# Router logits from the normalised attention output, turned by VectorE, in place of nine columns of values

## The chip, the core and the metric

The kernel runs on one core of a Trainium2 chip. The core has five engines that run side by side and meet at semaphores: TensorE (PE, with its weight loads shown apart as PEld), VectorE (DVE), ScalarE (ACT), GpSimd (POOL) and SyncE (SP, which here only issues DMAs). The metric is device time in microseconds for one execution, the median of the runs. Everything is float32.

## The reference

Attention over 8 batches, 8 heads, 576 positions and 64 features is followed by a mixture of 8 experts that sends each token to one expert:

```python
scores = q @ k.T / sqrt(D); cum = cumsum(max(s, 0))
scores = where(causal, -1e9, scores + min(-(cum[i] - cum[j]), 0))
x = softmax(scores) @ v                       # (B, H, S, D) -> (B, S, 512)
logits = x @ w_gate                           # 8 per token
local_gate = sigmoid(x @ w_local)             # 1 per token
e = argmax(logits) if s == 0 or local_gate < 0.5 else e of the token before
out = softmax(logits)[e] * (relu(x @ w1[e]) @ w2[e])      # 512 -> 1024 -> 512
```

A token's row of x is needed twice: for its nine router values (eight logits and the locality gate), and in its expert.

## The kernel before

**Attention.** A slot is one pair of heads; there are 32, four (`HP`) to a batch. The loop over `n` writes out by hand what each engine gets. In slot `n`, PE computes the scores of pair `n` in four units (`scores`, L896), each into a bank `ps` from a pool of three pairs of banks; ACT takes the exponential (L897), POOL masks the diagonal (L882). Then PE multiplies the weights of pair `n - 1` with the values (`values`, L923). The result `po` has 64 query rows of one head in partitions 0 to 63 and of the other in 64 to 127, and it is made in two parts, chunks 0 to 5 (`NJA`) and 6 to 8. `po` has one buffer for each part. `evacuate` on DVE takes the reciprocal of the sum column (L929), writes x into `xb` (L931) and, before the change, the nine router columns into `lb` (L933).

**Where the router values come from.** The product is linear, so the kernel before appends nine columns to the 64 of each head's values: v times the router weights of that head. A value row in `vg` has `VW` = 75 columns: 64 of v, nine router columns, and two for sums. To make them, v is also loaded in a turned layout (`vT`, `load_vT`), PE multiplies it with `wbd` (`value_logits`, L837, bank `vwp`), DVE turns the result into `tk` (L841, L843), and `weigh_logits` (L865) or `weigh_heads` (L879) multiplies it with the key weights. After a group of two batches `sums` adds the four pairs (L941) and `product` adds the two head halves on PE with the 0/1 matrix `fold` (L193, bank `lp`).

**The router's steps.** `codes` finds the best expert, `turn1` and `turn2` carry an expert along the tokens that keep it, `ranks` (PE) and `rows` give each token its row in a table in device memory, `gates` the probability, and 18 `scatter` calls a group put the rows of x there with indirect DMAs on POOL (L309), each behind a small operation on `gap` (L308) that waits for a given evacuation. Which step stands in which slot is written by `plan(slot, place, f)`: place 0 is behind score unit 1, place 1 behind the first part of the values, place 3 at the slot's end. `xb` has four buffers, one per batch, so a batch's buffer is rewritten four batches later, when its scatters have landed. For the last group these steps run inside the experts' first unit (`Experts.run`, the table `todo`), and scatters that are left over (`puts`) go one to each piece of the first layer.

**The experts.** After slot 32 the table's rows are fetched in units of up to 256 rows; PE runs the first layer (L539, L530) and the second (L563), while the weights of the next expert stream in.

**Other work in a slot.** `weigh` (L855) multiplies the v of the next batch with key weights on DVE, in three pieces; `load_qk` and `load_v` issue DMAs on SP. In the first two slots the order is special: v is weighed pair by pair (`weigh_heads` over `PARTS`).

Of the kernel before, what the change touches and what calls it, by code (L numbers as in the profile page):

```python
# [32 lines left out]
VW = DH + E + 3  # L33
WR = 16
NJ = S // DH
# [23 lines left out]
def kernel(  # L59
# [6 lines left out]
    vT: bass.AP,  # L66
# [3 lines left out]
    wbd: bass.AP,  # L70
# [15 lines left out]
    with ExitStack() as main:  # L86
        router = Router(main, tc, ident, table)
        experts = Experts(main, tc, w1, w2, out, table, router)
        with ExitStack() as early:
            attention(early, tc, q, k, vm, vt, vT, s, wbd, ident, recs, wend, router, experts)  # L90
        experts.run(recs, wend, out_of)
# [18 lines left out]
class Router:  # L110
# [8 lines left out]
    def constants(self):  # L119
        nc, ident, table = self.nc, self.ident, self.table  # L120
        self.fold = self.t("fold", [P, P])
        for h in range(2):
            nc.gpsimd.tensor_tensor(self.fold[:, h * DH : h * DH + DH], ident[:, :DH], ident[:, DH:], op=Alu.add)
# [59 lines left out]

    def t(self, name, shape, dt=F32):
        return self.const.tile(shape, dt, name=name)
# [4 lines left out]
    def product(self, g, ls, banks):  # L190
        flat = banks("lp")[:, 0, : NC * (E + 1)]
        ps = flat.rearrange("p (c e) -> p c e", e=E + 1)
        self.nc.tensor.matmul(flat, lhsT=self.fold, rhs=ls.rearrange("p c e -> p (c e)"),  # L193
                              start=True, stop=True)
        self.g[g] = {"l": ps}
# [217 lines left out]
class Experts:  # L413
    def __init__(self, ctx, tc, w1, w2, out, table, router):
# [11 lines left out]
        self.p_x = self.x_stack.enter_context(tc.tile_pool(name="p_x", bufs=2 * GB, side="right"))  # L426
        self.puts = []
# [148 lines left out]
    def run(self, recs, wend, out_of):  # L576
# [14 lines left out]
        def late_rows():  # L591
# [7 lines left out]
            (0, 2): [lambda: router.product(last, self.ls, self.banks), lambda: router.codes(last),  # L599
# [93 lines left out]
def attention(ctx, tc, q, k, vm, vt, vT, s, wbd_in, ident, recs, wend, router, experts):  # L693
# [9 lines left out]
    p_v = pool("p_v", 1)  # L703
    p_e = pool("p_e", 2)
    p_x = experts.p_x
    p_sm = pool("p_sm", 1)
# [6 lines left out]
    ins, vTs, es, xs, lgs = {}, {}, {}, {}, {}  # L713
# [16 lines left out]
    def load_vT(b):  # L730
        if b >= B:
            return
        vTs[b] = p_v.tile([P, HP, NB * P], F32, name="vTb")
        nc.sync.dma_start(vTs[b], vT[b])

# [11 lines left out]
    wbd = once.tile([P, HP, 2 * WR], F32, name="wbd")  # L747
    load_qk(1)
    nc.sync.dma_start(wbd, wbd_in)
    vTs[0] = p_v.tile([P, HP, NB * P], F32, name="vTb")  # L750
    for a0, a1 in PARTS:
        hs = slice(2 * a0, 2 * a1)
        nc.sync.dma_start(vTs[0][:, a0:a1], vT[0][:, a0:a1])
        nc.sync.dma_start(va[:, :NF, hs], vm[0][:, :, hs])
        nc.sync.dma_start(va[TL:, NF, hs], vt[0][:, hs])
    for n in range(2, 4):
        load_qk(n)
    wk1 = once.tile([P, B, G1, H], F32, name="wk1")
# [66 lines left out]
    def value_logits(b, a0=0, a1=HP):  # L825
        if b >= B:
            return
        vTb = vTs[b] if a1 < HP else vTs.pop(b)
        m, n = min(a1 - a0, HP - 1), 2 * WR
        ps = banks("vwp")  # L830
        pm = ps[:, 0, : m * NB * n].rearrange("p (a c e) -> p a c e", a=m, c=NB)
        pl = ps[:, 1, : NB * n].rearrange("p (c e) -> p c e", c=NB)
        for hp in range(a0, a1):
            at = vTb[:, hp, :].rearrange("p (c r i) -> p r c i", c=NB, r=4)
            for r in range(4):
                d = slice(32 * r, 32 * r + 32)
                mm(pm[d, hp - a0] if hp - a0 < m else pl[d], lhsT=wbd[:, hp, :], rhs=at[:, r], start=True, stop=True)  # L837
        if a0 == 0:
            lgs[b] = p_sm.tile([P, NB, HP, n], F32, name="tk")
        tk = lgs[b]  # L840
        nc.vector.transpose(tk[:, :, a0 : a0 + m].rearrange("p c a e -> p a c e"), pm)  # L841
        if a1 - a0 > m:
            nc.vector.transpose(tk[:, :, HP - 1], pl)  # L843

# [15 lines left out]
    def weigh_logits(b):  # L860
        if b >= B:
            return
        tk = lgs[b].rearrange("p c a (h e) -> p c (a h) e", h=2)
        for g, c in enumerate((G1, NB)):
            nc.vector.tensor_tensor(vgs[b % 2][g][:, :, :, DH : DH + E + 1].rearrange("p c h e -> p (c h) e"),  # L865
                                    tk[:, :c, :, : E + 1].rearrange("p c h e -> p (c h) e"),
                                    (wk1, wk2)[g][:, b].rearrange("p c h -> p (c h)").unsqueeze(2)
                                    .to_broadcast([P, c * H, E + 1]), op=Alu.mult)

    def weigh_heads(a0, a1, logits):  # L870

        hs = slice(2 * a0, 2 * a1)
        for g, c in enumerate((G1, NB)):
            to, of = vgs[0][g][:, :, hs, :DH], va[:, :c, hs]
            if logits:
                to = vgs[0][g][:, :, hs, DH : DH + E + 1]
                of = lgs[0].rearrange("p c a (h e) -> p c (a h) e", h=2)[:, :c, hs, : E + 1]
            w = (wk1, wk2)[g][:, 0, :, hs].unsqueeze(3).to_broadcast(list(to.shape))
            nc.vector.tensor_tensor(to, of, w, op=Alu.mult)  # L879
# [29 lines left out]
    def values(n, j0, j1):  # L909
# [4 lines left out]
        if (g, "l") not in xs:  # L914
            xs[g, "l"] = p_sm.tile([P, HP, NC, E + 1], F32, name="lb")
        xb, lb = xs[b], xs[g, "l"]
# [34 lines left out]
    for g in range(NG):  # L951
# [6 lines left out]
        if g == NG - 1:  # L958
            break
# [670 lines left out]
```

## Time and profile before

| what | value |
|---|---|
| median of 3 runs | 756.76 us (756.22 to 757.38) |
| profiled execution, its own time | 757.18 us |
| its span on the core | 755.4 us |
| first expert matmul | 232.75 us |
| busy PE, DVE, ACT, POOL | 98%, 31%, 22%, 28% of the span |
| granted TensorE clock | 0.997 |

The span is that of the program's own instructions, and 1.8 us of the profiled execution lie around it. A line of the profile names an engine, the source line, the operation and `out<-in` by the program's tile names; x is a count. A float32 matmul stands in the profile as two instructions, so counts of matmuls are twice those of the code. PE's busy time includes modelled ends of overlapping matmuls; for durations of a block, the start of the next block minus its own start is used.

### The profile page before, as it was taken

The page shows a single profiled execution, that of the slowest core. Times are in us where ns is not written, and L with a number is a line of the kernel's source. Part 1 is how long each engine was busy: PE and PEld are TensorE (multiplying, and loading weights), DVE is VectorE, ACT ScalarE, POOL GpSimd, SP SyncE. Part 2 cuts the span into 40 slices and gives each one's busy share as a digit, 9 for nine tenths or more (in the row PEclk, how much of TensorE's full clock was granted, in tenths as well). Part 3 has the DMA queues.
Part 4 walks back from the last instruction along what each step waited for, and adds up shares of the span by engine and source line. Part 5 has one row for each costly group of instructions (what it writes and reads, how often), then busy time and mean ns, then how long its engine had stood idle before and what let it go on. Part 6 is the DMA issues. An engine that isn't in the chain of part 4 may idle for free.

```text
span 755.4 us, 15982 instructions
## 1 busy us (share of the span) xinstructions
PE 743.3 (98%) x6463; PEld 511.8 (68%) x6463; DVE 236.7 (31%) x677; ACT 163.2 (22%) x319; POOL 214.7 (28%) x455
## 2 busy tenths in 40 slices
PE   8999999999999999999999999999999999999996
PEld 5888888887789567567567365637644676637674
DVE  4655655655656372101100411041132001050110
ACT  4544444443541011011011010201110111101110
POOL 2562376675657245340100011010101001000110
PEclk9999999999999999999999999999999999999998
DMA  8766457659677896598545979996999965899000
GB/s 279 263 244 228 159 174 273 207 176 315 217 254 271 270 373 215 210 422 233 213 177 169 374 246 392 339 378 242 423 321 383 410 220 216 297 391 354 29 14 33
DMA packets 56580, 196.50 MB, mean 260 GB/s; under 512 B 11693, under 2 KB 32429, under 8 KB 47280
## 3 DMA queue, kind: packets, MB, share of 16 engines
q1 hardware_dynamic: 49696, 175.28, 65.4%
q0 software_dynamic: 6800, 20.09, 7.0%
q8 instruction: 53, 0.87, 0.5%
q14 instruction: 31, 0.25, 0.1%
HBM read 174.73 MB, written 20.88 MB: 259 GB/s over the span
## 4 chain that ended last, share of the span: by engine, by line
PE 94%; DVE 2%; POOL 1%; DMA 1%; issue 1%; ACT 0%; POOLq 0%; ACTq 0%
PE yp L563 34%; PE hp L539 30%; PE po L923 13%; PE ps L896 11%; PE hp L530 4%; PE vwp L837 1%; DMA table<-xb,idx 1%; PE warm L770 1%; POOL e L882 0%; DVE vg L855 0%; DVE xb L931 0%; ACT e L897 0%; POOL table L309 0%; DVE mi L227 0%; PE pos L261 0%
## 5 line engine op out<-in xcount | busy, mean ns | idle before, releaser
L563 PE MATMUL yp<-w2b,hT 128*128 128x512 f32 (+2 forms) x752 | 259.3, 593 | 0.0
L539 PE MATMUL hp<-xT,w1b 128*128 128x256 f32 (+1 forms) x1216 | 233.1, 352 | 0.0
L539 PEld LDWEIGHTS hp<-xT,w1b 128*128 128x128 f32 x1216 | 206.2, 190 | 32.4 <-issue 7.3
L563 PEld LDWEIGHTS yp<-w2b,hT 128*128 128x128 f32 (+2 forms) x752 | 107.9, 167 | 141.0 <-issue 139.6
L568 POOL DMA_INDIRECT out_dram<-y,gi x37 | 36.2, 978 | 416.9 <-DVE y L566 386.7
L541 ACT ACTIVATE hT<-hp 128x256 f32<-128x256 f32 (+1 forms) x152 | 54.1, 356 | 430.2 <-PE hp L539 430.2
L566 DVE TENSOR_SCALAR y<-yp,gi 128x512 f32<-128x512 f32 x37 | 27.6, 746 | 309.9 <-PE yp L563 303.6
L897 ACT ACTIVATE e<-ps 128x768 f32<-128x768 f32 (+1 forms) x128 | 97.6, 836 | 108.3 <-PE ps L896 107.2
L923 PE MATMUL po<-vg,e 128*64 128x75 f32 x3200 | 113.3, 229 | 0.0
L923 PEld LDWEIGHTS po<-vg,e 128*64 128x64 f32 x3200 | 107.2, 136 | 3.8 <-issue 0.8
L896 PE MATMUL ps<-qb,kb 64*128 64x192 f32 (+4 forms) x768 | 99.8, 403 | 3.4 <-DVE u L206 1.9
L896 PEld LDWEIGHTS ps<-qb,kb 64*128 64x128 f32 x768 | 68.5, 188 | 35.1 <-ACT e L897 9.7
L309 POOL DMA_INDIRECT table<-xb,idx x72 | 75.7, 1051 | 28.2 <-issue 25.9
L882 POOL TENSOR_SCALAR_AFFINE_SELECT e<-e 128x256 f32<-128x256 f32 (+1 forms) x160 | 64.1, 427 | 52.3 <-ACT e L897 51.2
L550 DVE STREAM_TRANSPOSE hT<-hs 32x256 f32<-32x256 f32 x64 | 27.9, 436 | 74.9 <-ACT hs L532 74.0
L929 DVE RECIPROCAL recs<-po 128x12 f32<-128x12 f32 x64 | 13.2, 207 | 75.0 <-PE po L923 74.8
L931 DVE TENSOR_TENSOR xb<-po,recs 128x384 f32<-128x384 f32 x64 | 29.3, 458 | 7.1 <-DMA table<-xb,idx 4.8
L855 DVE TENSOR_TENSOR vg<-va,wk 128x1024 f32<-128x1024 f32 (+1 forms) x21 | 29.6, 1412 | 0.7 <-DMA va<-in_vm_dram 0.7
L509 DVE STREAM_TRANSPOSE xT<-xq 128x1024 f32<-128x1024 f32 (+1 forms) x23 | 23.7, 1032 | 15.2 <-DMA xq<-table 14.9
L530 PE MATMUL hp<-w1b,xT 128*32 128x512 f32 (+1 forms) x224 | 28.3, 594 | 0.0
L530 PEld LDWEIGHTS hp<-w1b,xT 128*32 128x32 f32 (+1 forms) x224 | 8.1, 114 | 17.7 <-issue 17.6
L308 POOL COPY gap<-recs 1x1 f32<-1x1 f32 x39 | 8.5, 217 | 29.4 <-DVE recs L929 29.2
(235 smaller groups left out, 188.1 us busy)
## 6 DMA issues: line engine op xcount, KB each, us to landing
w1b<-in_w_dram SPq DMA_DIRECT2D x29, 2048.0 KB
w2b<-in_w_dram SPq DMA_DIRECT2D x29, 2048.0 KB
kb<-in_k_dram SPq DMA_DIRECT2D x32, 288.0 KB
qb<-in_q_dram SPq DMA_DIRECT2D x32, 288.0 KB
vTb<-in_vT_dram SPq DMA_DIRECT2D x7, 1280.0 KB
xq<-table SPq DMA_DIRECT2D x56, 130.0 KB
va<-in_vm_dram SPq DMA_DIRECT2D x7, 1024.0 KB
w1b<-in_w_dram SPq DMA_DIRECT2D x4, 512.0 KB
```

The lines of the kernel that those rows point to most:

```text
L309: put = self.nc.gpsimd.indirect_dma_start(out=self.halves, in_=src, element_offset=0, in_offset=None, out_offset=bass.IndirectOffsetOnAxis ...
L530: mm(ps[d, :], lhsT=xT[:, k, d], rhs=self.ws[l][0][:, k, c * 512 : c * 512 + 512], start=(k == 0), stop=(k == DK - 1))
L539: mm(ps[:, :w], lhsT=self.ws[ls[0]][0][:, k, c * P : c * P + P], rhs=xT[:, k, :w], start=(k == 0), stop=(k == DK - 1))
L541: nc.scalar.activation(self.hT[u][:, c, :w], ps[:, :w], Act.Relu)
L563: mm(ps[d, :], lhsT=hT[:, k, n * P + d.start : n * P + d.stop], rhs=self.ws[l][1][:, k, :], start=(k == 0), stop=(k == FK - 1))
L568: put = nc.gpsimd.indirect_dma_start(out=self.out[:, :], out_offset=bass.IndirectOffsetOnAxis(ap=gi.bitcast(I32)[:, n, 0:1], axis=0), in_= ...
L855: nc.vector.tensor_tensor(vgs[b % 2][g][:, c0:c1].rearrange("p c h e -> p (c h) e")[:, :, :DH], va[:, c0:c1].rearrange("p c h e -> p (c h) ...
L882: nc.gpsimd.affine_select(out=ap, in_=ap, compare_op=Alu.is_ge, fill=0.0, base=base, pattern=n, channel_multiplier=-1)
L896: mm(ps[:, h, at : at + z - a], lhsT=kb[d, key : key + P], rhs=qb[d, a:z], start=True, stop=True)
L897: nc.scalar.activation(e, ps, Act.Exp, scale=scale)
L923: mm(po[d, j - j0, :], lhsT=weights_of(n, c, j, h), rhs=vg[:, c, 2 * hp + h, :], start=(c == 0), stop=(c == last))
L931: nc.vector.tensor_tensor(xb[:, j0:j1, :, 32 * hp : 32 * hp + 32], po[:, :, :DH].rearrange("p j (g i) -> p j g i", g=2), rec[:, :, 0].unsq ...
```

## The change

The values lose the nine router columns (`VW` is 66), and with them `vT`, `value_logits`, `weigh_logits`, `lb`, `sums` and `fold` go. Instead, after each pair's second evacuation `turn` transposes the pair's x on DVE in 32x32 blocks into `xt`. `product` multiplies that with the router weights `wx`: 32 matmuls a group (four pairs, two halves of 32 features, two batches, two runs of five chunks) that accumulate in one bank, each batch and run in its own group of 32 columns. `logits` turns the bank back and copies the nine values to where `codes` reads them. For the last group the product is split by batch: the first half in slot 29, the second in the experts' first unit. `codes` to `turn2` move to later places, some scatters to earlier ones, the loads of v by one slot, and two score units of the second pair behind the first values.

```diff
-VW = DH + E + 3
+VW = DH + 2
+NJH = 5
...
-        self.fold = self.t("fold", [P, P])
-        for h in range(2):
-            nc.gpsimd.tensor_tensor(self.fold[:, h * DH : h * DH + DH], ident[:, :DH], ident[:, DH:], op=Alu.add)
...
-    def product(self, g, ls, banks):
-        flat = banks("lp")[:, 0, : NC * (E + 1)]
-        ps = flat.rearrange("p (c e) -> p c e", e=E + 1)
-        self.nc.tensor.matmul(flat, lhsT=self.fold, rhs=ls.rearrange("p c e -> p (c e)"),
-                              start=True, stop=True)
-        self.g[g] = {"l": ps}
+    def product(self, g, xts, banks, bs=range(GB)):
+
+        ps = self.g.setdefault(g, {})["lp"] = banks("lp")[:, 0, : NJH * 32]
+        i = 0
+        for hp in range(HP):
+            for d in range(2):
+                for b in bs:
+                    for c in range(2):
+                        at = 32 * (2 * b + c)
+                        j = c * (NJ - NJH)
+                        self.nc.tensor.matmul(ps[at : at + 32], lhsT=self.wx[:, hp, d],
+                                              rhs=xts[b][:, hp, d, j : j + NJH].rearrange("p j t -> p (j t)"),
+                                              start=(i == 0), stop=(i == 2 * HP - 1))
+                i += 1
+
+    def logits(self, g, bs=range(GB)):
+        v = self.nc.vector
+        st = self.g[g]
+        p = slice(DH * bs[0], DH * bs[-1] + DH)
+        lt = self.s("lt", [P, NJH, 2, WR])
+        v.transpose(lt[p].rearrange("p j q e -> p (j q e)"), st.pop("lp")[p])
+        if "l" not in st:
+            st["l"] = self.s("l", [P, NC, E + 1])
+        l = st["l"]
+        for b in bs:
+            for c in range(2):
+                j = b * NJ + c * NJH
+                skip = c * (2 * NJH - NJ)
+                for r in range(2):
+                    at = 32 * (2 * b + c)
+                    v.tensor_copy(l[32 * r : 32 * r + 32, j : j + NJH - skip],
+                                  lt[at : at + 32, skip:, r, : E + 1])
+        c = slice(bs[0] * NJ, bs[-1] * NJ + NJ)
+        v.tensor_copy(l[DH:, c], l[:DH, c])
...
-            (0, 2): [lambda: router.product(last, self.ls, self.banks), lambda: router.codes(last),
+            (0, 2): [lambda: router.product(last, self.xts_of, self.banks, (1,)),
+                     lambda: router.logits(last, (1,)), lambda: router.codes(last),
                      lambda: router.turn1(last), lambda: router.turn2(last)],
...
+    router.projection(wx)
...
-            nc.vector.tensor_tensor(lb[:, hp, o + j0 : o + j1, :], po[:, :, DH : DH + E + 1],
-                                    rec[:, :, 0].unsqueeze(2).to_broadcast([P, m, E + 1]), op=Alu.mult)
...
+    def turn(n):
+
+        b, hp = divmod(n, HP)
+        bl = b % GB
+        if hp == 0:
+            xts[b] = (p_xt, experts.p_xt)[bl].tile([P, HP, 2, NJ, 32], F32, name=f"xt{bl}")
+        nc.vector.transpose(xts[b][:, hp].rearrange("p d j t -> p j d t"), xs[b][:, :, :, 32 * hp : 32 * hp + 32])
...
-        plan(n, 3, first)
-        if g == NG - 1:
-            break
-        plan(n + 1, 1, lambda g=g: router.product(g, of[g][1], banks))
-        plan(n + 1, 1, lambda g=g: router.codes(g))
-        plan(n + 2, 1, lambda g=g: router.turn1(g))
-        plan(n + 3, 1, lambda g=g: router.turn2(g))
+        plan(n + 1, 1, lambda g=g: router.product(g, of(g), banks))
+        plan(n + 1, 1, lambda g=g: router.logits(g))
+        plan(n + 2, 1, lambda g=g: router.codes(g))
+        plan(n + 3, 1, lambda g=g: router.turn1(g))
+        plan(n + 3, 3, lambda g=g: router.turn2(g))
         plan(n + 4, 1, lambda g=g: router.ranks(g, banks))
...
-            if m - n in (6, 8, 10) and m < NPAIR:
+            if m - n in (5, 6, 7) and m < NPAIR:
                 places.append((m, 0))
...
+    n = NPAIR - HP + 1
+    plan(n, 1, lambda: router.product(NG - 1, (xts[B - 2],), banks, (0,)))
+    plan(n, 1, lambda: router.logits(NG - 1, (0,)))
...
-            weigh_heads(*PARTS[0], False)
+            weigh_heads(*PARTS[0])
             scores(1, 1)
-            value_logits(0, *PARTS[0])
-            weigh_heads(*PARTS[0], True)
-            scores(1, 2)
-            scores(1, 3)
             continue
...
         if n == 1:
-            weigh_heads(1, 2, False)
-            value_logits(0, *PARTS[1])
-            weigh_heads(1, 2, True)
-        if hp == 0:
-            load_vT(b + 1)
-        if hp == 1 and b:
-            weigh(b + 1, 1, 0, 3)
-        if hp == 2 and b:
-            weigh(b + 1, 1, 3, NB)
-        if hp == 3:
-            if b:
-                weigh_logits(b + 1)
+            scores(1, 2)
+            scores(1, 3)
+            weigh_heads(1, 2)
+        if b:
+            if hp == 1:
+                weigh(b + 1, 1, 0, 3)
+            if hp == 2:
+                weigh(b + 1, 1, 3, NB)
                 load_v(b + 2)
-            else:
-                weigh(1, 1, 0, 3)
-        evacuate = values(n - 1, NJA, NJ)
-        if hp == 2:
-            value_logits(b + 1)
-        evacuate()
+        elif hp == 3:
+            weigh(1, 1, 0, 3)
+        values(n - 1, NJA, NJ)()
+        turn(n - 1)
```

The range check at the end (`in_range`) reuses one tile for two, with the same operations.

## The prediction

> **What bounds the kernel now.** I read the busy shares first, then TensorE's two stages by window, then the chain and TensorE's waits, then single steps on the timeline. PE is busy for 98% of the span, and the windows (columns: length, then PE, PEld, DVE, ACT, POOL busy) show it on both sides of the hand-over at 232.75 us, where the first expert matmul starts:
>
> ```profile
> PE 743.3 (98%) x6463; PEld 511.8 (68%) x6463; DVE 236.7 (31%) x677; ACT 163.2 (22%) x319; POOL 214.7 (28%) x455
> ```
> ```profile
> 0.00:232.75 232.75, 227.49 (x4261) 188.41 (x4262) 133.09 (x423) 104.02 (x158) 133.27 (x309) 1.00 0.68 229
> 232.75:755.40 522.65, 515.79 (x2205) 323.38 (x2202) 103.61 (x254) 59.22 (x161) 81.47 (x147) 1.00 0.75 274
> ```
>
> The reader is to see that no other engine comes near PE: in attention DVE and POOL are at 133 us of 233. The expert stage is idle for 6.86 us in all, which is the tail after the last matmul. Its matmuls are not touched, so the change can win or lose only where it alters PE's own queue in attention, or a wait in it.
>
> The chain of waits between 100 and 180 us gives the price of each item of that queue (start, us, what):
>
> ```profile
> 108.39 1.23 PE vwp L837 x32
> 109.61 2.95 PE ps L896 x24
> 112.57 3.43 PE po L923 x100
> 116.00 2.95 PE ps L896 x24
> ...
> 127.04 0.47 PE lp L193 x2
> ```
>
> A plain slot is one pair of heads: 2.95 us of scores and 3.43 us of weighted values, 6.38 us. Once per batch there is 1.23 us of value logits, once per group 0.47 us of fold. PE's waits up to 233 us are few:
>
> ```profile
> PE ps L896 <- DVE u L206: 1.9, 1, 1.9
> PE ps L896 <- DVE recs L929: 1.0, 2, 0.6
> PE ps L896 <- ACT e L897: 0.5, 2, 0.3
> ```
>
> The large one is at 185 us. On PE and on DVE the timeline shows (start, busy us, engine line, idle before):
>
> ```profile
> 182.72 0.54 PE L193 MATMUL lp<-ls,fold 128*128 128x162 f32 x2
> 185.05 1.88 PE L896 MATMUL ps<-qb,kb 64*128 64x384 f32 x12
> 188.81 1.02 PE L896 MATMUL ps<-qb,kb 64*128 64x448 f32 x4 [1.88 <-DVE u L206]
> ```
> ```profile
> 187.35 0.56 DVE L931 TENSOR_TENSOR xb<-po,recs 128x384 f32<-128x384 f32 x1 [4.29 <-DMA table<-xb,idx]
> 188.50 0.17 DVE L206 TENSOR_SCALAR u<-lp 128x18 f32<-128x18 f32 x1
> ```
>
> DVE may not overwrite a buffer of x until its scatter has landed; it stands 4.29 us; behind it are the three readers of bank lp, and PE's scores need that bank. The scores took 6.00 us there. They took 3.16, 3.61 and 3.84 us at 81.6, 136.9 and 195.7 us, where bank vwp was released late: 0.21 + 0.66 + 3.05 + 0.89 = 4.8 us over 2.95.
>
> **The change, part by part.**
>
> (a) Narrower values, 75 to 66 columns. A pair has 100 records, two heads side by side in the two column halves, so 50 steps of 3.43 / 50 = 68.6 ns. The price of a column is read where only the width differs, late in the expert stage:
>
> ```profile
> 706.34 7.31 PE L539 MATMUL hp<-xT,w1b 128*128 128x128 f32 x64
> 713.48 7.03 PE L563 MATMUL yp<-w2b,hT 128*128 128x512 f32 x16
> 720.35 0.83 PE L539 MATMUL hp<-xT,w1b 128*128 128x128 f32 x6
> ```
>
> From start to start, 64 records of 128 columns take 7.14 us, 111.6 ns each; 16 of 512 take 6.87 us, 429.4 ns. (429.4 - 111.6) / 384 = 0.83 ns a column; nine columns are 7.5 ns of a step, 0.37 us a pair, 12.0 us over 32 pairs. This holds if the weight load doesn't become the limit. The rows of the value products are:
>
> ```profile
> L923 PE MATMUL po<-vg,e 128*64 128x75 f32 x3200 | 113.3, 229 | 0.0
> L923 PEld LDWEIGHTS po<-vg,e 128*64 128x64 f32 x3200 | 107.2, 136 | 3.8 <-issue 0.8
> ```
>
> Here the Trainium skill speaks against the change: Perfetto Trace Analysis, section Identifying the Most-Contended Engine, takes the busy share of the weight loads, not of the matmuls, as the measure of what TensorE has left. By that only 113.3 - 107.2 = 6.1 us is to be had, and my sum would be 5.9 us smaller. I take the trace's rates instead: a load record of 128 columns lasts 190 ns on the page, yet its matmuls of 128 columns follow each other every 111.6 ns, so records overlap and their union is no rate. Half the columns should load in about 56 ns, under the 61.1 ns that a step would last. The ends are 0 (loads already bind) and 12.0 us; I take 12.0.
>
> (b) Value logits out: seven of 1.22 us, and 0.41 and 0.95 us at the start: -9.9 us.
>
> (c) Fold out: three of 0.47 us and one of 0.28 us in the expert stage: -1.7 us.
>
> (d) New products, same shape as the value logits (128x32 weights, 160 columns, 32-column groups side by side). Eight records there took 0.41 us, 32 took 1.22: (1.22 - 0.41) / 6 = 0.135 us for a step of four, plus 0.14 us. A group has 64 records, 16 steps: 2.30 us, three times. The last group is split by batch; each half fills only two of the four column groups, so its 32 records need 16 steps too: 2 x 2.30. Together +11.5 us. If two fp32 passes of one product did not overlap with neighbours, each product would need twice the steps, +11 more; the value rows, which accumulate too, do overlap, so I take no extra.
>
> (e) The start. From 12.21 to 18.88 us PE ran both value logits, second scores and the first values. Now the first values come straight after scores unit 1, and must wait for DVE's first weighing of v (12.39 us on, 0.42 us for its 128x256 part): about 0.6 us of idle PE that the logits covered. Below nothing isn't excluded (v lands sooner); I take +0.5.
>
> (f) Old waits. No bank vwp, so 0.21, 0.66 and 0.89 have nothing to wait for. The scatter that held DVE is chunk 8 of its group; it moves from slot n+8 to n+7, and its buffer is rewritten at n+9. Measured landings are 3 to 7 us around 180 us, and one slot is over 6, so the 3.05 goes as well: -4.8 us; the other end is 0.
>
> (g) New waits. DVE loses the lb pass (12.1 us), the tk transposes (7.9), weighing of logits (7.6) and the sums (5.1), 32.7 us. It gets 32 transposes of 128x576 and the logits:
>
> ```profile
> L509 DVE STREAM_TRANSPOSE xT<-xq 128x1024 f32<-128x1024 f32 x14 | 17.4, 1243 | 12.8 <-DMA xq<-table 12.5
> L509 DVE STREAM_TRANSPOSE xT<-xq 128x512 f32<-128x512 f32 x9 | 6.3, 703 | 2.3 <-DMA xq<-table 2.3
> L235 DVE COPY ei<-exm 32x18 f32<-32x18 f32 x16 | 2.9, 182 | 0.2
> ```
>
> Between those widths a turn is 0.77 us, 24.6 us in all; logits are a 0.30 us transpose, eight copies near 0.19 and one of some 0.3: 2.1 us a group, 8.4 in all. So +33.0 against -32.7: DVE stays at 133 us of some 218. Its worst place is slot n+3: evacuation, turn1 (1.6 us), second evacuation, turn (0.77), turn2 (2.5) end about 10.7 us after the slot's start, and PE wants their result for the ranks at 6.0 + 4.5 = 10.5. That is up to 0.3 us, three times. On POOL the puts crowd: three in each of slots n+5 to n+7, 1.35 to 1.68 us each (gap 0.18, issue 0.15 to 0.5, issue of the DMA 1.0), with five masks of 0.35 to 0.45: 5.9 to 7.1 us against a slot of 6.0. PE reads masks one slot later, which covers some 3 us; past that each us of lag is a us of PE. ACT's exponential for the router no longer stands in the slot of the product. SP loses the vT loads (8 x 1.28 MB), gets wx (128 KB instead of 64) behind q and k, and loads v one slot earlier: no engine waited for those. Ends of (g): 0 to +6; I take +1.5.
>
> Sum: -12.0 - 9.9 - 1.7 + 11.5 + 0.5 - 4.8 + 1.5 = -14.9 us. The profiled execution took 757.18 us (span 755.4); it becomes 742.3. It stood 0.4 us over the median of the runs shown, 756.76, so the median becomes 741.9.
>
> **Rivals.** (1) Weight loads bind the values: the step falls to 64 to 68 ns and (a) gives 1 to 7 us, not 12; time 747 to 753. For it: the load row as full as the matmul row; against it: 111.6 ns for 128-column loads. (2) New waits eat the gain: masks late behind the crowded puts, ranks late behind turn2, or the landing still holding DVE; (g) at +6 or (f) at zero: 746 to 750. For it: puts already delay masks in the chain near 177 us; against it: a slot of slack. (3) Slower: DVE becomes the bound through the turn, whose write scatters 32-element runs. Without it DVE has 133 - 25 = 108 us over 32 slots, 3.4 us each; the old slot averaged 232.75 / 32 = 7.3. It turns slower once a turn takes over 3.9 us; at 4.4 it would be 7.8 us a slot, +16 us, 773. Against it: 1.24 us for a permuted transpose almost twice as wide. (4) The change doesn't do what it says: the products don't overlap, +11 us in (d): 753.
>
> **How the numbers follow.** The sum's own case, gain 12 to 17 us: 0.67 (740 to 745). Rival 1: 0.12. Rival 2: 0.12. Rival 3: 0.04. Rival 4: 0.05. About 0.2% (1.5 us) is what a measurement of this kernel can tell from no change. Faster by more: all of the first three and most of the fourth, less something for a cost I do not see, 0.91; within 0.02; slower 0.07. The range takes in the first case with both old and new waits at their good ends (739) and rival 2 (750).
>
> **What would show it.** Right: po at some 3.05 us a pair; lp runs of 2.3 us at three places; scores at 2.95 us after each; expert stage again 522 to 525 us with its product of 2.3; turns near 0.77 us. Wrong: po steps of 64 ns or more (rival 1); PE waiting for POOL e or for DVE before ranks (rival 2); turns above 2 us (rival 3); lp over 4 us (rival 4). An expert stage waiting for weights would break the frame itself.

## The result and the profile after

The changed kernel takes 745.18 us (median of 4 runs, 744.71 to 745.22); the kernel before took 756.54 us beside it (4 runs, 756.22 to 757.38). The ratio is 0.9847, with a 95% interval of 0.983 to 0.9864: 11.4 us faster by the medians. The forecast was 741.9 in a range of 739 to 750. The direction and the mechanism hold, and the gain is 3.5 us short of the 14.9 foretold. The profiled execution took 744.71 us (span 743.0); it was the fastest of its four, and that of before, at 757.18 us, lay above its median, so the two spans lie 12.4 us apart.

The busy shares first (engine, us, share, instructions), then the two stages by window, cut at the first expert matmul (length, then busy us of PE, PEld, DVE, ACT and POOL, then clock, DMA share, GB/s):

```profile
PE 730.5 (98%) x6455; PEld 501.7 (68%) x6455; DVE 246.4 (33%) x647; ACT 162.2 (22%) x319; POOL 211.2 (28%) x453
```
```profile
0.00:218.23 218.23, 212.51 (x4223) 176.60 (x4223) 142.28 (x388) 103.25 (x158) 131.79 (x309) 1.00 0.61 197
218.23:743.00 524.77, 518.01 (x2236) 325.14 (x2232) 104.10 (x259) 58.97 (x161) 79.36 (x145) 1.00 0.74 272
```

Attention ends at 218.23 instead of 232.75 us, 14.52 us sooner; the expert stage is 2.12 us longer, of which 2.02 are its half of the last group's product (2.30) less the fold that stood there (0.28). So nearly the whole question lies in PE's queue before 218 us. That queue, on the chain between 160 and 180 us (start, us, what):

```profile
165.35 2.95 PE ps L884 x24
168.31 1.55 PE po L909 x48
169.86 2.31 PE lp L201 x64
172.17 1.67 PE po L909 x52
173.83 2.95 PE ps L884 x24
176.79 3.07 PE po L909 x100
```

Scores keep their 2.95 us. A pair's values are now 3.07 us instead of 3.43, and the new product (`lp`) takes 2.31 us once per group. Two groups of instructions carry the rest (shapes, count | busy us, mean ns | idle before, and who ended it):

```profile
L909 PE MATMUL po<-vg,e 128*64 128x66 f32 x3200 | 102.7, 224 | 1.6 <-POOL e L870 0.9 <-DVE vg L866 0.7
L909 PEld LDWEIGHTS po<-vg,e 128*64 128x64 f32 x3200 | 96.8, 138 | 6.1 <-POOL e L870 2.0
...
L927 DVE STREAM_TRANSPOSE xt<-xb 128x576 f32<-128x576 f32 x32 | 24.9, 778 | 1.1
```

The load row fell with the matmul row, from 107.2 to 96.8, though no weight load changed: its busy time follows the matmuls, and was no floor for them at 75 columns. A turn costs 0.778 us. PE's waits before 230 us (us in total, times, longest):

```profile
PE pos L289 <- DVE recs L915: 2.0, 3, 0.7
...
PE po L909 <- POOL e L870: 0.9, 1, 0.9
PE po L909 <- DVE vg L866: 0.7, 1, 0.7
```

All waits of scores for DVE are gone. In their place PE waits three times for DVE ahead of the ranks (`pos`), and once for POOL's mask. Block by block, from start to start (us):

| block | before | after | difference |
|---|---|---|---|
| up to the first full scores run of 24 records | 18.88 | 17.23 | -1.65 |
| scores | 93.39 | 88.59 | -4.80 |
| values, 31 pairs | 107.08 | 99.86 | -7.22 |
| value logits | 8.57 | 0 | -8.57 |
| fold or product | 1.42 | 9.23 | +7.81 |
| ranks, group ends | 3.41 | 3.33 | -0.08 |
| expert stage | 522.65 | 524.77 | +2.12 |

The values gained 7.22 where 31 pairs at 0.36 us less should have given some 11.2. Most of the difference is in five runs: the 48 records before the ranks took 2.17, 2.36 and 2.37 us where the others take 1.55 (+2.25 in all), the values of slot 24 took 3.32 (+0.25), and the last, double run 7.12 where 5.95 was to be expected from a pair and most of another (+1.2). What makes PE wait at the three ranks is seen on DVE's timeline in the first group (start, busy us):

```profile
82.01 0.78 DVE L927 STREAM_TRANSPOSE xt<-xb 128x576 f32<-128x576 f32 x1
82.71 0.80 DVE L264 COPY ei<-exm 32x18 f32<-32x18 f32 x4
...
85.25 0.54 DVE L280 TENSOR_TENSOR_SCAN incl<-seg,hot 128x144 f32<-128x144 f32 x1
```

The new turn stands ahead of `turn2` (L264 to L280), whose last result `incl` is what the ranks read. What holds the last run, on POOL and PE:

```profile
211.40 0.18 POOL L337 COPY gap<-recs 1x1 f32<-1x1 f32 x1 [2.57 <-DVE recs L915]
212.08 0.98 POOL L338 DMA_INDIRECT table<-xb,idx  x1 [0.51 <-issue]
...
213.79 0.09 POOL L335 MEMSET gap<- 1x1 f32 x1
214.04 0.99 POOL L338 DMA_INDIRECT table<-xb,idx  x1 [0.17 <-issue]
215.04 1.01 POOL L870 TENSOR_SCALAR_AFFINE_SELECT e<-e 128x256 f32<-128x256 f32 x3
215.52 2.65 PEld L909 LDWEIGHTS po<-vg,e 128*64 128x64 f32 x88 [1.06 <-POOL e L870]
```

POOL works in order. A scatter of slot 30's end stands 2.57 us for an evacuation, and the one that the change put at place 0 of slot 31 (213.79 to 215.03; behind a `MEMSET` it waits for no evacuation) takes 1.2 us more ahead of the last three masks, which PE needs. The first wait is there without this scatter too (2.58 us in e3, below, and in e8).

### The profile page after: what moved, and what is told of

It reads as the page before. It is cut to its first block, busy times and chain, and to the rows that moved or that the text cites. A ratio compares the mean times of both kernels' runs of the same rounds, so it can differ in the third digit from the quotient of the medians.

```text
span 743.0 us, 15903 instructions
## 1 busy us (share of the span) xinstructions
PE 730.5 (98%) x6455; PEld 501.7 (68%) x6455; DVE 246.4 (33%) x647; ACT 162.2 (22%) x319; POOL 211.2 (28%) x453
## 4 chain that ended last, share of the span: by engine, by line
PE 94%; DVE 3%; POOL 0%; issue 0%; POOLq 0%
PE yp L593 35%; PE hp L569 31%; PE po L909 12%; PE ps L884 11%; PE hp L560 4%; PE lp L201 2%; DVE xb L916 0%; DVE ei L264 0%; DVE xt L927 0%; DVE recs L915 0%; POOL table L338 0%; DVE incl L280 0%; PE pos L290 0%; PE pos L289 0%; POOL e L870 0%
## 5 line engine op out<-in xcount | busy, mean ns | idle before, releaser
L909 PE MATMUL po<-vg,e 128*64 128x66 f32 x3200 | 102.7, 224 | 1.6 <-POOL e L870 0.9
L909 PEld LDWEIGHTS po<-vg,e 128*64 128x64 f32 x3200 | 96.8, 138 | 6.1 <-POOL e L870 2.0
L884 PE MATMUL ps<-qb,kb 64*128 64x192 f32 (+4 forms) x768 | 97.5, 400 | 0.2 <-ACT e L885 0.2
L338 POOL DMA_INDIRECT table<-xb,idx x72 | 73.8, 1025 | 22.3 <-issue 20.4
L870 POOL TENSOR_SCALAR_AFFINE_SELECT e<-e 128x256 f32<-128x256 f32 (+1 forms) x160 | 65.9, 438 | 45.5 <-ACT e L885 44.7
L539 DVE STREAM_TRANSPOSE xT<-xq 128x1024 f32<-128x1024 f32 (+1 forms) x23 | 23.6, 1028 | 14.9 <-DMA xq<-table 14.6
L927 DVE STREAM_TRANSPOSE xt<-xb 128x576 f32<-128x576 f32 x32 | 24.9, 778 | 1.1
```

The costliest lines, as they stand in the source:

```text
L338: put = self.nc.gpsimd.indirect_dma_start(out=self.halves, in_=src, element_offset=0, in_offset=None, out_offset=bass.IndirectOffsetOnAxis ...
L870: nc.gpsimd.affine_select(out=ap, in_=ap, compare_op=Alu.is_ge, fill=0.0, base=base, pattern=n, channel_multiplier=-1)
L884: mm(ps[:, h, at : at + z - a], lhsT=kb[d, key : key + P], rhs=qb[d, a:z], start=True, stop=True)
L909: mm(po[d, j - j0, :], lhsT=weights_of(n, c, j, h), rhs=vg[:, c, 2 * hp + h, :], start=(c == 0), stop=(c == last))
```

## Experiments

Twelve kernels ran on three chips. The kernel before had medians of 755.22, 758.76 and 754.86 us on them. The columns give the start (first full scores run), the end of attention, the length between, and the values' sum in the profiled execution; the changed kernel of the first trace is the first row. Every row but that of e9 has four runs or more.

| kernel | chip | median | ratio (95%) | start | end | between | values |
|---|---|---|---|---|---|---|---|
| changed, first trace | - | 745.18 | 0.9847 (0.983-0.9864) | 17.23 | 218.23 | 201.00 | 99.86 |
| e1_wide76 | 1 | 755.17 | 0.9998 (0.998-1.0015) | 18.00 | 228.64 | 210.64 | 109.48 |
| e2_turn_last | 1 | 743.25 | 0.9845 (0.9825-0.9866) | 17.66 | 217.29 | 199.63 | 98.45 |
| e3_puts_late | 1 | 747.13 | 0.9912 (0.9882-0.9943) | 16.92 | 218.59 | 201.67 | 100.20 |
| e4_assign_late | 1 | 745.69 | 0.9881 (0.9861-0.9902) | 17.70 | 219.05 | 201.35 | 100.19 |
| e5_changed_again | 2 | 752.77 | 0.9925 (0.9896-0.9953) | 17.18 | 226.06 | 208.88 | 107.72 |
| e6_vT_back | 2 | 755.68 | 0.9966 (0.9948-0.9985) | 18.63 | 228.95 | 210.32 | 108.04 |
| e7_four_groups | 2 | 753.19 | 0.9928 (0.9902-0.9954) | 17.81 | 226.09 | 208.28 | 107.31 |
| e8_no_put31 | 2 | 751.72 | 0.9916 (0.9886-0.9947) | 16.52 | 225.60 | 209.08 | 107.81 |
| e9_before_again | 3 | 757.32 (one run) | - | 18.71 | 232.87 | 214.16 | 106.83 |
| e10_best | 3 | 742.30 | 0.9838 (0.9825-0.9852) | 18.19 | 215.80 | 197.61 | 97.26 |
| e11_turn_twice | 3 | 750.12 | 0.9939 (0.9924-0.9954) | 18.62 | 223.91 | 205.29 | 104.13 |
| e12_changed_third | 3 | 745.69 | 0.9879 (0.9864-0.9895) | 18.65 | 219.57 | 200.92 | 99.78 |

The start wanders between 16.5 and 18.7 us with nearly the same code there, so "between" is the better measure of one edit. The changed kernel itself did not run on chip 1; e1 to e4 are set against its first trace, run by run. The three runs ahead of the ranks were 2.17, 2.36 and 2.37 us there, and the same within 0.01 in e4 and e12.

### What the narrower values are worth

Each value row is read as 76 columns, two overlapping runs of 38; ten columns come twice.

```diff
-                                      rhs=vg[:, c, 2 * hp + h, :],
+                                      rhs=doubled(vg[:, c, 2 * hp + h, :]),
...
+    def doubled(a):
+        return bass.AP(a.tensor, a.offset, [list(a.ap[0]), [28, 2], [1, 38]])
```

> The changed kernel, but each value matmul again moves 76 columns instead of 66 (28 to 37 of each head's row are streamed twice; the doubled results are not read). Nothing else differs, so it prices the narrowing alone. My theory (a value step is bound by the moving columns, 0.83 ns each): a step of 57.8 + 10 x 0.83 = 66 ns, a pair of 3.5 us, and about 11.5 to 13 us more than the changed kernel, 757 to 758 us. Rival (weight loads already bind at 66 columns, so that narrowing was only partly paid): a step under 64 ns and less than 9 us more. Second rival (waits on other engines hide in the longer steps): steps of 66 ns, but the waits for ranks and masks shrink and the total rises by only 9 to 10 us.

The chain of waits of this kernel:

```profile
105.83 2.95 PE ps L885 x24
108.79 3.44 PE po L913 x100
...
121.58 1.73 PE po L913 x48
123.31 2.31 PE lp L202 x64
```

A pair is back at 3.44 us. From 3.07 that is 0.37 us for ten columns in 50 steps, 0.74 ns a column; the nine columns of the change gave (3.43 - 3.07) / 50 / 9 = 0.80 ns. Weight loads are unchanged in all three, so they do not set the pace at 75 or 76 columns; at 66 a step is 61.4 ns, where the price of a column had given 61.1, so little can be hidden there either. The values' sum rose by 9.62 us, not by 31 x 0.37 = 11.5: the waits ahead of the ranks shrank from 2.25 us to 1.2, as is to be expected where a longer step gives DVE more time before PE asks, and the last run lost some 0.6 us of its wait. With ten columns more, one more than the change took away, nothing is left of the gain (ratio 0.9998): all the rest of the change together about pays for itself.

### The new wait before the ranks

In the slots whose number leaves 3 when divided by 8, the turn goes behind `turn2`.

```diff
-        turn(n - 1)
+        if n % (HP * GB) != 3:
+            turn(n - 1)
...
         at(n, 3)
+        if n % (HP * GB) == 3:
+            turn(n - 1)
```

> The changed kernel, but in slots n+3 of a group (11, 19, 27) the turn of the pair's x stands behind turn2 instead of before it on VectorE. My theory: TensorE's three waits before the ranks (0.6, 0.8 and 0.8 us by the lengths of the value runs ahead of them) come from turn2 being finished 0.78 us later because of that turn; then they shrink to under 0.1 us each and the total falls by 1.8 to 2.2 us. Rival (VectorE is late by more than the turn, because its small copies run slower beside GpSimd): the waits fall by 0.78 us at most and some 0.1 to 0.3 us stay; or the delayed turn pushes the first evacuation of the next slot and the wait reappears behind it: no gain.

PE's waits before 230 us in this kernel:

```profile
PE warm L791 <- DVE xb L767: 1.5, 1, 1.5
PE po L909 <- POOL e L870: 1.2, 2, 0.9
PE po L909 <- DVE vg L866: 0.7, 1, 0.7
...
PE po L909 <- DVE xb L916: 0.3, 1, 0.3
```

The list begins with the warm-up at the start; the line for `pos`, which stood above it, is gone. The 48-record runs took 1.55, 1.66 and 1.66 us: 2.0 of the 2.25 us are back. Attention between start and end is 1.4 us shorter than in the first trace, not 2.0, since some 0.6 us came in other value runs (slot 24 went from 3.32 to 3.56, slot 5 to 3.53). The cause of the rank waits is shown: with the turn behind `turn2` they are nearly gone, and `turn2` itself got no shorter (3.09 to 3.39 us).

### The scatters, first explanation of the old 3.05 us

The three extra scatters of a group go to slots n+6, n+8 and n+10 instead of n+5, n+6 and n+7, which puts chunk 8 later again.

```diff
-            if m - n in (5, 6, 7) and m < NPAIR:
+            if m - n in (6, 8, 10) and m < NPAIR:
```

> The changed kernel, but the extra scatters stand in slots n+6, n+8 and n+10 again, as before the change. If the moved scatters removed the old wait for a landing (DVE 4.3 us, TensorE 3.05 us in slot 25), it comes back: scores in slot 25 of 5 to 6 us. If it was the product's later reading of lp, or one transpose that frees the bank, that removed it, slot 25 stays at 2.95 us although DVE waits for the landing. For the end of attention: if the put in slot 31 delays the last masks, the last values (7.12 us) fall to about 6.0 us here, because that put is gone. So my theory says +3 - 1.1 = about +2 us; the rival about -1 us.

No wait of DVE for a landing came back, and the scores of slot 26, the ones that took 6.00 us (the expectation calls the slot 25), stay at 2.95 us. The prediction's reason for that part of the gain, that chunk 8 was moved one slot ahead, falls. Two other things showed. The end of attention, by the chain of waits:

```profile
209.72 2.95 PE ps L884 x24
212.68 5.98 PE po L909 x200
```

With no scatter at place 0 of slot 31 the last values take 5.98 us instead of 7.12, so the extra scatters were the cause there; e8 takes out the one of slot 31 alone. And the waits ahead of the ranks grew in groups two and three (48-record runs of 3.39 and 3.16 us instead of 2.36), perhaps because scatters left over now crowd those slots; that was not tried alone. The edit as a whole gains nothing.

### A later assignment

```diff
-    plan(n + 7, 1, lambda: router.assign_early(0))
+    plan(n + 7, 3, lambda: router.assign_early(0))
...
-    plan(n + 14, 1, lambda: router.assign_early(1))
+    plan(n + 14, 3, lambda: router.assign_early(1))
```

> The changed kernel, but both early assignments (slots 23 and 30, 3.8 us of small VectorE operations each) stand at the slot's end, behind the second evacuation and the turn, instead of ahead of them. My theory: the assignment delays the reciprocal that GpSimd's gap copy waits for; masks queue behind that copy, and TensorE's last values wait 0.9 us and more for them; then the last values take about 6.0 us instead of 7.1, slot 24's values 3.07 instead of 3.32, and the total falls by 1.2 to 1.5 us. Rival (the crowded puts alone make the masks late): the last values stay over 6.8 us and the total falls by less than 0.4 us.

The values of slot 24 went from 3.32 to 3.07 us. The last run got worse, 7.81 us. The wait changed its name, from POOL's mask to DVE:

```profile
PE po L909 <- DVE recs L915: 1.6, 1, 1.6
```

As a remedy for the last run the theory falls; the wait moved. Between start and end it is 0.35 us longer than the first trace.

### The same kernel on another chip

No edit.

> The changed kernel itself, once more, on the chip of the next three, so that they have it beside them: some 10 to 12 us under the kernel before.

Here the changed kernel gained 6.0 us by the medians and not 11.4. Scores are 88.62 us and the product 9.23, as before; the whole difference is 7.9 us in the values, and all of it in slots 13 to 32, the time of the scatters. The chain of waits there:

```profile
99.09 0.28 issue
99.38 1.88 PE po L909 x55
...
105.66 0.29 issue
105.95 1.32 PE po L909 x31
107.27 0.37 issue
```

Inside a run of values PE stops for about 0.3 us and waits for nothing that the profile shows. In the stretch shown the masks and the scatters are no later than in the first trace. Nor does loading of instructions explain it: both traces have the same 98 packets of the instruction queues (1.18 MB), and from 105 to 107.8 us, where two of the gaps lie, these queues carry nothing.

### The turned loads of v, second explanation of the 3.05 us

The late scatters of e3, and the eight vT loads of the kernel before issued again, into a buffer that nothing reads.

```diff
+    def load_vT(b, a0=0, a1=HP):
+        if b < B:
+            c = slice(a0 * NB * P, a1 * NB * P)
+            nc.sync.dma_start(spare[:, c], vT[b].rearrange("p a t -> p (a t)")[:, c])
...
+        if hp == 0:
+            load_vT(b + 1)
```

> The changed kernel with the extra scatters at n+6, n+8 and n+10 as before, and with the loads of the turned v put back at the places they had before (1.28 MB a batch, into a tile that nothing reads). It differs from the run with late scatters by these loads alone. In that run VectorE's wait for a landing did not come back, so my first explanation (the scatters were moved) fell. New theory: the landing was late because the load of the turned v in slot 24 filled the DMA engines; then the scatter of chunk 8 lands in 5 to 7 us instead of 2.6, VectorE waits again in slot 25 (1 to 4 us), and the start is some 0.4 us later too. Rival (the later slots have simply shifted against the loads of weights): landing stays at 2.5 to 4 us and no wait comes back.

DVE's waits:

```profile
DVE xb L925 <- DMA table<-xb,idx: 2.5, 3, 2.0
```

The longest of them, in slot 25, and PE's scores of slot 26 behind it:

```profile
177.79 0.56 DVE L925 TENSOR_TENSOR xb<-po,recs 128x384 f32<-128x384 f32 x1 [2.04 <-DMA table<-xb,idx]
...
179.52 3.02 PE L893 MATMUL ps<-qb,kb 64*128 64x384 f32 x24
...
182.47 3.54 PE L918 MATMUL po<-vg,e 128*64 128x66 f32 x100
```

The wait of DVE for a landing is back, 2.0 us for chunk 8 of a group. The scatter was issued at 170.15, so DVE could go on 7.6 us after the issue; in e3, without these loads, it had landed after 3.2 us, but that was on the other chip. PE pays nothing for it: the scores of slot 26 start at 179.52 and take 2.95 us. Longer scores stand elsewhere, in slots 19, 27 and 29 (0.29, 0.40 and 0.42 us more), and e3 has 0.16 and 0.17 us of this in slots 19 and 27 without the loads. The start is 1.45 us later than in e5, but e12, which has none of these loads, has the same start (18.65 against 18.63). So the loads that the change removes may bring back a part of DVE's wait, with the chip as an untested rival. That their removal took away PE's 3.05 us, or made the start earlier, is not shown. An untested explanation is that DVE now reads bank lp once (`lt`, 0.35 us) where three readers stood before. A second trace of the kernel before (e9, below) shows how loose the size is.

### The last group's product in four column groups

Each half of the last group's product uses all four column groups, in runs of three chunks, instead of two groups in runs of five.

```diff
+        return [(b, 32 * i, j, b * NJ + j + skip, skip, 3) for b in bs
+                for i, (j, skip) in enumerate(((0, 0), (3, 0), (5, 1), (6, 2)))]
```

> The changed kernel, but the two halves of the last group's product use all four column groups: three chunks each instead of five in two groups. Steps of four with 96 columns: 16 x (0.83 x 96 + 3) ns + 0.14 = 1.47 us a half instead of 2.30, 0.8 us twice; two more logits copies each on VectorE, off the path. Theory: total 1.6 to 1.7 us less, lp runs of 1.45 us at the two places. Rival (a step cannot go under the 0.136 us that any such step took, because of weight loads): runs stay at 2.3 us, no gain.

On the second chip the halves took 2.10 and 1.64 us instead of 2.30 each, and the time is that of the changed kernel (753.19 against 752.77 us). The first half holds a gap:

```profile
204.18 0.94 PE lp L206 x34
205.12 0.26 issue
205.38 0.91 PE lp L206 x29
```

Here the run did not answer the question; e10 repeats this edit on another chip.

### No extra scatter in slot 31

```diff
-            if m - n in (5, 6, 7) and m < NPAIR:
+            if m - n in (5, 6, 7) and m < NPAIR - 1:
```

> The changed kernel without the extra scatter at place 0 of slot 31 (it goes to the experts' stage). With late scatters the last values took 5.98 us instead of 7.12; that run had neither this put nor the one in slot 29. Theory: this one put, which stands ahead of the last three masks and behind a gap copy that waits for VectorE's early assignment, is the cause: last values of 6.0 us, total 1.1 us less. Rival (the put in slot 29 is as guilty, GpSimd is late by the sum): 6.4 to 7 us.

The last values went from 8.75 to 7.97 us, 0.78 less. The run ahead of the third ranks went from 2.37 to 2.99 us. Between start and end nothing is gained (209.08 against 208.88), and the two intervals overlap. On this chip the trial is inconclusive.

### The kernel before, a second trace

No edit.

> The kernel before the change, unaltered, for a profile on the chip of this call. Question: on the second chip the changed kernel needed 7.9 us more in its value products than on the first, in gaps of 0.3 to 0.6 us that the chain of waits calls issue, all of them in the period of the scatters; the kernel before was there 3.5 us longer by its median. If the chip makes these gaps whatever the kernel, they stand in this trace too where the chip of this call is such a chip: its 75-column value runs in slots 13 to 31 above 3.43 us, by 0.1 to 0.5 each, 3 to 4 us in all. If they belong to the narrow products alone (a step of 58 ns leaves less slack for whatever feeds TensorE's queue than one of 65 ns), the value runs of this kernel stay at 3.41 to 3.43 us but for the last. On a chip like the first, no gaps are expected in either kernel and nothing is told apart.

On this chip, the third, the kernel has no gaps inside the value runs, which stay at 3.40 to 3.44 us but for the last. So the question about the second chip is not answered. But PE's waits from 150 to 210 us show something else:

```profile
...
PE ps L896 <- DVE u L206: 0.2, 1, 0.2
```

PE's wait for `u`, the last reader of lp, is here 0.2 us and not 1.9, and the scores of that slot took 4.00 us and not 6.00. DVE stood 2.3 us before it and not 4.3, and the profile names POOL's copy of `gap` as what ended that wait, so here even the landing as its cause is not certain. The span is nevertheless 755.6 against 755.4 us, because two "issue" gaps (1.2 and 1.4 us, at 33 and 40 us) fell into other scores. This execution took 757.32 us; the other nine on this chip took 753.67 to 755.78. So the 3.05 us of the first trace was 1.05 in this one; a wait for a DMA seen in one execution is a sample.

### Four edits together

The turn last (e2), the first assignment at place 3, no extra scatter in slot 31 (e8) and four column groups (e7).

```diff
+        if n % (HP * GB) == 3:
+            turn(n - 1)
...
+            if m - n in (5, 6, 7) and m < NPAIR - 1:
...
+    plan(n + 7, 3, lambda: router.assign_early(0))
```

> The changed kernel with four edits together: the turn behind the other vector work in slots with n mod 8 equal to 3 (removed 2.0 us of waits before the ranks), no extra scatter in slot 31 (0.8 to 1.2 us of the last values), the first assignment at place 3 (slot 24, 0.25 us), and the last group's product in four column groups (0.9 us). If these waits are separate, the sum is 3.9 to 4.3 us: ratio to the kernel before about 0.979 on a chip like the first (741), 0.987 on one like the second. If the waits move elsewhere when one is taken away, as the assignment's did, no more than 2 us is left of it. Rows: 48-record value runs before the ranks at 1.55 to 1.7 us, last values run 6.0 to 6.3 us on a chip like the first.

742.30 us against 745.69 for the changed kernel on the same chip (e12): 3.4 us, just under the expected 3.9 to 4.3; the absolute 741 was short by 1.3. The chain of waits near the end of attention:

```profile
195.38 1.55 PE po L910 x48
196.93 1.46 PE lp L206 x64
...
203.31 3.07 PE po L910 x100
206.38 0.48 issue
...
209.89 5.98 PE po L910 x200
215.87 5.38 PE hp L570 x24
221.25 1.46 PE lp L206 x64
```

The rank waits are nearly gone (-2.04 us against e12), the last run is at 5.98 (-1.16), each half product at 1.46 (-0.84, one of them in the expert stage). A 0.48 us gap and 0.3 us behind the first half product were lost. This is the lowest median of all; its ratio of 0.9838 does not part it from that of e2, 0.9845, on another chip.

### Every turn twice

```diff
-        nc.vector.transpose(xts[b][:, hp].rearrange("p d j t -> p j d t"), ...)
+        for _ in range(2):
+            nc.vector.transpose(xts[b][:, hp].rearrange("p d j t -> p j d t"), ...)
```

> Every turn is issued twice, into the same tile: 32 more VectorE instructions of 0.78 us, 25 us more of busy VectorE in attention (142 to 167 of about 220 us), nothing else altered. Prices the room on VectorE, which the third rival of the prediction was about. If VectorE has room as the prediction held, most is hidden: only the turns ahead of the ranks' work and of the crowded scatters cost, 0.8 us at about three places each, so 2 to 4 us over the changed kernel. If VectorE were near to setting the pace, each second turn would show in part: 10 us or more, with waits of TensorE for VectorE at most slots (value runs above 3.07 us, lp runs above 2.31).

Attention in this kernel as a window, and the first of PE's waits:

```profile
0.00:223.91 223.91, 214.07 (x4223) 177.85 (x4224) 166.28 (x419) 103.50 (x158) 134.29 (x309) 0.99 0.60 192
...
PE pos L289 <- DVE recs L915: 4.5, 3, 1.7
```

DVE is busy for 166 of 224 us, and 25 us more work there cost 4.4 us: 2.5 before the ranks (runs of 2.82, 3.29 and 3.28 us against 2.17, 2.37 and 2.37), and one gap of 1.9 us in a value run at 111 us, put down to issue. The other value runs are nearly those of the changed kernel. The four runs of this kernel lie within 0.6 us, and its median is 4.4 us above that of e12, so the gap is hardly an accident of the one traced execution; what makes it is open. DVE had room: most of the 25 us is hidden, and the part with a known cause is paid where PE waits for a chain on DVE.

### The changed kernel, third chip

No edit.

> The changed kernel unaltered, as the partner of the other runs of this call and to see how its gain depends on the chip: ratio 0.985 on the first chip, 0.9925 on the second. Expected: one of the two again, with the value runs of slots 13 to 31 at 3.07 us (attention's end at 218) or at 3.3 to 4.4 us (end at 226). A ratio between them with few gaps would speak for a graded cause, such as how fast instructions or descriptors come from memory, rather than for two kinds of chip.

Value runs at 3.07 us, end of attention at 219.57, waits as in the first trace; ratio 0.9879 (0.9864 to 0.9895). By the medians on this chip it gained 9.2 us, by the two profiled spans, 755.6 and 744.6 us, 11.0 (the trace of before is the slow one of e9). So the changed kernel gained 11.4, 6.0 and 9.2 us in its three comparisons; the trace of the third is that of the first, and only the second shows the gaps. The ratio lies between the two that were named, but not through gaps: the changed kernel has its first time again (745.69 against 745.18), and it is the kernel before that was quicker here (754.86 against 756.54). So a graded cause gets no support from it.

## Why the prediction was right, and where it was short

Predicted sum -14.9 us; between the two profiled spans -12.4. By the medians it was 11.4, just short of the 12 to 17 us of the sum's own case. Term by term:

- **(a) Narrower values, -12.0.** The mechanism holds, and the size nearly: the values gave -7.2 with 3.7 us of new waits in them, so -10.9 without, and about -11.2 with the first pair. The column cost 0.80 ns, not the 0.83 read from the wider expert matmuls. The first rival, steps of 64 ns or more, is out (61.4). The Trainium skill (Perfetto Trace Analysis, Identifying the Most-Contended Engine) judges TensorE's headroom by the busy share of the weight loads, beside the FLOPs done against the peak. Read off the load row as in the prediction, that left at most 6.1 us; these runs gave 10.9, and the load row shrank with the steps.
- **(b), (c) Value logits and fold out, -9.9 and -1.7.** As foretold: 8.57 and 1.36 at the start, 1.42 and 0.28.
- **(d) New products, +11.5.** Measured 2.31, 2.31, 2.31, 2.30 and 2.30 us, 11.53: the passes overlap, and the fourth rival is out.
- **(e) The start, +0.5.** About +0.1 in the first trace (18.88 to 17.23 us, of which 1.36 are the logits and 0.35 the narrower first pair), but in e12 against e9 there was no gain at all (18.71 to 18.65), which makes it +1.7. The value lies inside its own wander.
- **(f) Old waits gone, -4.8.** Measured -4.80 between these two traces. The size is partly luck: the second trace of the kernel before held 2.8 us of these waits. The reason given for the 3.05 was wrong (e3). The loads of vT brought back 2.0 us of DVE's wait and nothing of PE's (e6), so what took the 3.05 us away is open.
- **(g) New waits, +1.5.** This is the mis-sized term: it measured 3.7. "Up to 0.3 us, three times" ahead of the ranks became 0.62, 0.81 and 0.82. The step that failed is the length of `turn2`: the prediction put 2.5 us, while from the first `ei` copy to the end of `incl` the two traces show 2.72 to 2.79 us before and 3.08 to 3.27 after. The 2.5 was short even of the trace of before. Those 0.6 to 0.8 us come on a chain that was already put 0.2 us late; it reached `turn2` 0.3 us sooner than reckoned (7.92 us after the slot's start), and 0.15 us pass between the end of `incl` and the matmul, which makes the 0.6 to 0.8 us of wait. That the turn stands in that chain and makes the wait is shown by e2; why `turn2` grew is open. Masks behind crowded scatters were named, but not placed: they cost 1.2 us at the last run and 0.25 in slot 24.
- **DVE at 133 us.** It is 142 in the shorter stage. The sum of the instructions' own times rose by 1.5 us only (149.0 to 150.5), near the 0.3 foretold; the busy row counts overlapping records once, and rose by 9.2. The price of the turn was right (0.77 against 0.778), and e11 shows that the third rival was never near.

The terms as measured (-11.2 - 9.9 - 1.7 + 11.5 + 0.1 - 4.8 + 3.7) make -12.3, which closes on the -12.4; as (a) was found by taking (g) out of the values' sum, this checks the bookkeeping and not the split of the two. The second rival, new waits that eat the gain, was right in kind and took 2.2 us more than the main case allowed. What no term foresaw is the second chip, where another 5 us of the gain is missing; its place is measured (gaps in the value runs during the scatters), its cause is open. With 752.77 us there, the range of 739 to 750 would not have held: that the result fell into it is partly the luck of the chip. The kernel before was 3.5 us slower there too, but no trace of it on that chip says where.

## What to carry to other kernels

When a step on the bounding engine is shortened, list every chain on the other engines that ends in that engine's next operand, take each chain's length from start to end on the timeline of before, not from a sum of single instructions, and compare it with the new, shorter deadline; a shorter step moves the deadline forward by itself. Put new work on a side engine behind such a chain and not ahead of it: three turns a run came with 2.25 us of wait in one place and 0.2 in the other. A wait for a DMA that one trace shows should enter a sum with a second trace's value beside it.

## What the runs showed of the hardware that was not expected

- The same program lost 7.9 us of the values' time on the second chip, in PE gaps of about 0.3 us with no releaser, at a granted clock of 0.997. Single gaps of that kind, 0.5 to 1.9 us, stand in traces of the other chips as well (e9, e10, e11).
- Small DVE copies vary. The 32x18 `ei` copies took 0.12 to 0.17 us wherever POOL was idle (29 copies in ten traces). Beside a mask or the issue of a scatter on POOL many took the same, but others 0.2 to 0.7; in the first trace after the longest was 0.52. Whether POOL is the cause was not tried.
- Four column groups of 96 columns do 64 records in 1.46 us, two of 160 columns do 32 in 2.30, and four of 160 do 64 in 2.31: filling the column groups pays although twice as many instructions are issued.
